# Two convolutions on one core: the last stage's matrices block diagonal over two channel groups instead of four, applied as pairs of 64x64 array tiles

## The chip, the cores and the metric

One core of one Trainium2 chip. The metric is the device time of one execution in microseconds (us). A kernel is timed several times in turn with the kernel before on the same chip. The profile of a run is of one execution; its span is about 2 us shorter than the time of the same run.

## The reference, cut to what matters

Two long convolutions over 2048 steps of 448 channels, one with a filter that has to be generated from 256 complex modes a channel (A), one with a given filter (B), mixed by a gate:

```python
def reference(A_u, A_A_re, ..., B_ssm_D, gate_w):
    ...
    K = jnp.einsum("dn,dnl,dn->dl", Cc, P, dB).real        # A: the filter from its modes
    y = irfft(rfft(u, 4096) * rfft(K, 4096))[:2048] + u * Dskip
    ...
    y = irfft(rfft(kv, 4096) * rfft(ssm_k, 4096))[:2048]   # B; kv: a short convolution of k, times v
    ...
    x = A_u
    g = _sigmoid((x * gate_w).sum(-1, keepdims=True))
    return g * a + (1 - g) * b
```

(The transforms and the paddings are written in short here; the cuts are marked with dots.)

## The kernel before

The 448 channels are worked in four quarters H of 112 (28 columns by 4 groups g). Each transform is a chain of small matrix stages on TensorE (PE): stage c spreads the input over 32 frequencies (`spread`, ps_c), stage 2 (`transform`, ps), a product of spectra on VectorE (DVE, zs and zsS times zsK), and back through stage a (ps_a into U) and stage b, the last, into ps_b. The filter of A is made in eight **filter blocks**, two for each quarter: powers of the modes multiplied and added on DVE (kg_P, kg_TQ, kg_TP), then summed over the modes on PE (pk). A **convolution step** carries one quarter of A or B through the stages. The program emits step after step with a filter block each; a scheduler with a model of its own then sets the order on each engine.

The stage in question, and how its matrices are built. `g` runs over the four groups of a quarter. Column block g of a 128x128 matrix (32 columns) is nonzero only in the 32 rows that carry the same group (every fourth row), so three quarters of the matrix are zeros:

```python
    def stage_b(self, pool, qt, hqt, k_col, mask):                 # once, early
        G = pool.tile([P, 64, 2, 4, 32], bf16, name="sb_G")
        for b0 in range(0, 64, 16):
            ...                                                    # phases, then ACT: v = sin(...)
            for g in range(4):
                nc.vector.tensor_scalar(out=G[:, b0:b0 + 16, :, g, :], in0=v[:], scalar1=mask[:, g:g + 1], scalar2=None, op0=ALU.mult)

def stage_b(nc, psum, G, U, consume, banks=2):                     # eight times
    n = 16 * banks
    for b0 in range(0, 64, n):
        pt = psum.tile([P, banks, 512], f32, name="ps_b", tag="ps")
        for i in range(n):
            b = b0 + i
            o = pt[:, i // 16, (i % 16) * NC:(i % 16 + 1) * NC]
            for r in range(2):
                nc.tensor.matmul(o, lhsT=G[:, b, r].rearrange("p g a -> p (g a)"), rhs=U[:, r, b], start=(r == 0), stop=(r == 1))
        consume(b0, n, pt[:, :, 0:448])        # DVE: ug (B) or ept and ug (A), from ps_b; for one quarter ACT: y
```

## Time and profile before

| | before |
|---|---|
| time, median of 3 | 326.08 us (326.0 to 326.8) |
| span of the profiled run | 323.5 us |
| mean granted PE clock | 0.800 |
| last kg_TP ends / copy of kg_S begins | 284.6 / 291.6 us |
| the eight ps_b stages, from first to last matmul | 28.7 us in all, 3.2 to 4.6 each |

How to read it: DVE is the busiest engine until the last filter block, so the time can be written as a **ledger of DVE**: what passes before the first filter operation (kg_P), DVE's work and idle time from there to the last kg_TP, and work and idle time in the tail behind it. The windows view: its columns are the stretch in us, its length, the busy time (and instructions) of PE, PE's weight loads, DVE, ACT and POOL, the granted clock, the DMA share and GB/s.

```profile
80.60:284.60 204.00, 160.99 (x4267) 148.48 (x4265) 193.18 (x377) 174.41 (x304) 9.42 (x1) 0.82 0.17 37
284.60:323.50 38.90, 19.22 (x565) 17.84 (x563) 11.82 (x22) 12.58 (x17) 0.00 (x0) 0.66 0.34 64
```

DVE idles 204.0 - 193.2 = 10.8 us in the stretch and 38.9 - 11.8 = 27.1 us in the tail. The chain that ended last, by line:

```profile
ACT zs L565 12%; PE ps_b L279 7%; PE pk L371 6%; ACT ET L481 6%; ACT U L565 5%; ACT zsK L565 5%; PE ps_c L215 5%; SPq L634 4%; POOL skraw L592 4%; PE ps L227 3%; SPq L587 3%; PE ps_a L265 3%; ACT ET L493 3%; SPq L631 2%; ACT ET L511 2%
```

### The profile page before, as it was taken

To read this page: it belongs to the slowest core of one execution; us is meant where nothing else is said; L and a number is where in the kernel's file an instruction comes from. 1 tells how busy PE (TensorE), PEld (TensorE's weight loads), DVE (VectorE), ACT (ScalarE), POOL (GpSimd) and SP (SyncE) were. 2 spreads that over 40 slices of the span, in tenths; PEclk is the share of its full clock that TensorE was granted. 3 is DMA by queue.
4 is the path that set the end of the run, shared out by engine and by line. 5 is a ranking of instruction groups with operands and counts; after the bars stand their busy time and mean duration, and the time that the engine had idled before them with its cause. 6 is when DMAs were issued, how large, how long until landed. Compare 5 with 4: busy or idle time off the path is not lost.

```text
span 323.5 us, 11944 instructions
## 1 busy us (share of the span) xinstructions
PE 225.5 (70%) x5286; PEld 197.4 (61%) x5286; DVE 277.2 (86%) x571; ACT 243.2 (75%) x395; POOL 34.6 (11%) x129
## 2 busy tenths in 40 slices
PE   0498617737278678699997857999774779966740
PEld 0144607237167568588886846998674678865740
DVE  7999999967999899979999998988999889942450
ACT  3655888779991799998989999689989474936600
POOL 9400002912000009000000000000000000000000
PEclk9999855796758767967997975899998559995765
DMA  6889999730000530050040015004000500040048
GB/s 129 137 188 152 165 164 168 239 59 0 2 0 4 117 57 3 5 158 2 4 102 19 4 45 116 3 4 97 22 2 4 115 3 4 12 108 2 2 91 140
DMA packets 53740, 21.41 MB, mean 66 GB/s; under 512 B 49080, under 2 KB 52024, under 8 KB 53688
## 3 DMA queue, kind: packets, MB, share of 16 engines
q1 hardware_dynamic: 48936, 19.47, 31.6%
q10 hardware_dynamic: 4560, 1.15, 2.0%
q8 instruction: 41, 0.67, 0.9%
q14 instruction: 11, 0.09, 0.1%
q0 software_dynamic: 192, 0.03, 0.1%
HBM read 10.09 MB, written 3.21 MB: 41 GB/s over the span
## 4 chain that ended last, share of the span: by engine, by line
ACT 39%; PE 26%; SPq 14%; DVE 9%; POOL 4%; issue 3%; DMA 3%; ACTq 0%; DVEq 0%; POOLq 0%
ACT zs L565 12%; PE ps_b L279 7%; PE pk L371 6%; ACT ET L481 6%; ACT U L565 5%; ACT zsK L565 5%; PE ps_c L215 5%; SPq L634 4%; POOL skraw L592 4%; PE ps L227 3%; SPq L587 3%; PE ps_a L265 3%; ACT ET L493 3%; SPq L631 2%; ACT ET L511 2%
## 5 line engine op out<-in xcount | busy, mean ns | idle before, releaser
L565 ACT CAST zs<-ps_c 128x1024 bf16<-128x1024 f32 (+1 forms) x48 | 42.5, 940 | 4.8 <-PE ps_c L215 4.7
L227 PEld LDWEIGHTS <-s_W 128*128 128x128 bf16 x480 | 34.4, 118 | 16.7 <-issue 14.2
L318 DVE TENSOR_TENSOR kg_P<-kg_TQ,ET 128x896 bf16<-128x896 bf16 (+1 forms) x64 | 43.8, 705 | 0.3
L565 ACT CAST zs<-ps 128x896 bf16<-128x896 f32 x48 | 41.4, 929 | 1.6 <-PE ps L227 1.5
L227 PE MATMUL ps<-zs,s_W 128*128 128x112 bf16 x384 | 32.2, 252 | 12.2 <-ACT zs L565 6.3
L371 PE MATMUL pk<-kg_TP,kg_TQ 128*21 128x32 bf16 x1792 | 30.3, 238 | 8.5 <-issue 6.3
L371 PEld LDWEIGHTS <-kg_TQ 128*21 128x21 bf16 x1792 | 27.8, 121 | 10.3 <-issue 9.6
L265 PE MATMUL ps_a<-sa_R,zs 128*128 128x128 bf16 x196 | 29.0, 240 | 6.8 <-ACT U L565 4.5
L592 POOL TENSOR_TENSOR skraw<-skraw,dB 128x28 bf16<-128x28 bf16 x4 | 23.3, 5816 | 94.9 <-DMA skraw<-in_B_ssm_k_dram 94.9
L565 ACT CAST U<-ps_a 128x1024 bf16<-128x1024 f32 (+2 forms) x32 | 29.3, 947 | 3.5 <-PE ps_a L253 1.8
L318 DVE TENSOR_TENSOR kg_P<-kg_TP,ET 128x1792 bf16<-128x1792 bf16 (+1 forms) x32 | 30.8, 963 | 0.0
L279 PEld LDWEIGHTS <-sb_G 128*128 128x128 bf16 x1024 | 27.9, 99 | 3.9 <-issue 3.6
L279 PE MATMUL ps_b<-U,sb_G 128*128 128x28 bf16 x1024 | 28.1, 179 | 2.9 <-ACT U L565 1.3
L265 PEld LDWEIGHTS <-zsS 128*128 128x128 bf16 x196 | 26.2, 153 | 5.2 <-issue 5.2
L265 PE MATMUL ps_a<-sa_R,zsS 128*128 128x128 bf16 x196 | 28.5, 239 | 0.0
L265 PEld LDWEIGHTS <-zs 128*128 128x128 bf16 x196 | 26.2, 152 | 2.6 <-DVE zs L286 1.7
L323 DVE TENSOR_TENSOR kg_TQ<-kg_P 128x896 bf16<-128x896 bf16 (+2 forms) x64 | 27.7, 442 | 0.2
L493 ACT ACTIVATE ET<-ks_ph 128x448 bf16<-128x448 int16 x40 | 23.8, 603 | 5.0 <-DVE ks_ph L489 4.0
L565 ACT CAST zsK<-ps_c 128x512 bf16<-128x512 f32 (+2 forms) x28 | 22.1, 798 | 7.0 <-PE ps_c L215 6.9
L215 PE MATMUL ps_c<-WcK,kg_KT 128*64 128x128 bf16 x224 | 19.9, 305 | 9.1 <-ACT zsK L565 5.8
L655 PE MATMUL ps_v<-kvt,scratch 128*128 128x448 bf16 x64 | 16.3, 387 | 13.5 <-DVE kvt L651 13.1
L215 PE MATMUL ps_c<-Wc,kv 128*64 128x128 bf16 x224 | 15.6, 321 | 14.1 <-DVE kv L680 7.8
(141 smaller groups left out, 481.4 us busy)
## 6 DMA issues: line engine op xcount, KB each, us to landing
zsS<-zs SPq DMA_DIRECT2D x16, 448.0 KB, 5.6
kt<-in_B_k_dram SPq DMA_DIRECT2D x16, 112.0 KB, 4.3
skraw<-in_B_ssm_k_dram SPq DMA_DIRECT2D x16, 112.0 KB, 3.6
vt<-in_B_v_dram SPq DMA_DIRECT2D x4, 448.0 KB, 6.8
uu<-in_A_u_dram SPq DMA_DIRECT2D x4, 448.0 KB, 8.7
xfd<-ks_hold SPq DMA_DIRECT2D x2, 672.0 KB, 6.9
ks_xf<-xfd SPq DMA_DIRECT2D x3, 336.0 KB, 3.0
out_dram<-ug SPq DMA_DIRECT2D x8, 112.0 KB, 4.8
```

The lines of the kernel that those rows point to most:

```text
L215: nc.tensor.matmul(pt[64 * r:64 * r + 64, i, :], lhsT=x, rhs=W[:, 128 * r:128 * r + 128], start=True, stop=True, tile_position=(0, 64 * r))
L227: nc.tensor.matmul(pt[:, i // 4, (i % 4) * n:(i % 4 + 1) * n], lhsT=W[:, k].rearrange("p r s -> p (r s)"), rhs=zs[:, k], start=True, stop= ...
L265: nc.tensor.matmul(pt[:, i, :], lhsT=t[:].rearrange("p k (g c) -> p (k g) c", g=4)[:, :, j + i], rhs=R[:, 128 * n:128 * n + 128], start=(n ...
L279: nc.tensor.matmul(o, lhsT=G[:, b, r].rearrange("p g a -> p (g a)"), rhs=U[:, r, b], start=(r == 0), stop=(r == 1))
L318: put(V.tensor_tensor(out=P4[:, i:i + m].rearrange("p n v c m -> p n v (c m)"), in0=in0, in1=in1, op=ALU.mult))
L323: put(V.tensor_tensor(out=T[:, dst:dst + v.shape[1] // 2].rearrange("p n v m -> p (n v) m"), in0=v[:, :, 0], in1=v[:, :, 1], op=ALU.add))
L371: nc.tensor.matmul(pt[32 * g:32 * g + NQ, hw, :].rearrange("p (i j) -> p i j", i=2), lhsT=TQ[:, :, c, m], rhs=rhs, start=(hf == 0 and c == 0),
L481: ex = nc.scalar.activation(dst, x, ACT.Exp, scale=float(e))
L493: sn = nc.scalar.activation(dst.rearrange("p b c m -> p b (c m)"), low16(ph[:].rearrange("p b c m -> p (b c m)")).rearrange("p (b x) -> p ...
L565: return nc.scalar.copy(dst, src)
L592: nc.gpsimd.tensor_tensor(out=raw[:, :, 0], in0=raw[:, :, 0], in1=dB[:, H * NC:(H + 1) * NC], op=ALU.add)
L655: nc.tensor.matmul(pt[:, i, 0:448], lhsT=ident, rhs=t[:, n, 4 * i:4 * i + 4, :].rearrange("p b l -> p (b l)"), start=(n == 0), stop=(n == 3))
```

## The change

The intent: not to build and load all of those zeros. With the four groups put into two halves h (two groups on partitions 0 to 63, two on 64 to 127), the halves never mix, so two of the four 64x64 blocks of the matrix are zero as a whole. The two others can run as independent tiles of the array, side by side, with half the matrix to build and to load. The cost is twice as many load and matmul instructions in the stage. Spectra (zs, zsS, zsK) are stored with the half outermost.

```diff
-        G = pool.tile([P, 64, 2, 4, 32], bf16, name="sb_G")
+        G = pool.tile([P, 64, 2, 2, 32], bf16, name="sb_G")
...
-            for g in range(4):
+            for g in range(2):
                 nc.vector.tensor_scalar(out=G[:, b0:b0 + 16, :, g, :], ...)
...
             for r in range(2):
-                nc.tensor.matmul(o, lhsT=G[:, b, r].rearrange("p g a -> p (g a)"), rhs=U[:, r, b], start=(r == 0), stop=(r == 1))
+                for h in range(2):
+                    q = slice(64 * h, 64 * h + 64)
+                    nc.tensor.matmul(o[q], lhsT=G[q, b, r].rearrange("p g a -> p (g a)"), rhs=U[q, r, b], start=(r == 0), stop=(r == 1),
+                                     tile_position=(64 * h, 64 * h))
...
-        zs = qt([P, 32, 4 * NC], "zs")
+        zs = qt([P, 2, 32, 2 * NC], "zs")
```

Cut: the same renaming of axes in `spread`, `transform`, `half_of`, `stage_a` and the copies, the spread matrix Wc built in two operations, and the columns of the mask.

More of the change, by code (lines that the diff above doesn't have):

```diff
@@ L109, in stage_c @@
         W = self.pool.tile([P, 256], bf16, name=name)
-        nc.vector.tensor_tensor(out=W[:].rearrange("p (n g) -> p n g", g=4), in0=v[:].unsqueeze(2).to_broadcast([P, 64, 4]),
-                                in1=maskg[:].unsqueeze(1).to_broadcast([P, 64, 4]), op=ALU.mult)
+        for h in range(2):
+            nc.vector.tensor_tensor(out=W[:].rearrange("p (r h k g) -> p h r k g", r=2, h=2, g=2)[:, h],
+                                    in0=v[:].rearrange("p (r k) -> p r k", r=2).unsqueeze(3).to_broadcast([P, 2, 32, 2]),
+                                    in1=maskg[:, 2 * h:2 * h + 2].unsqueeze(1).unsqueeze(1).to_broadcast([P, 2, 32, 2]), op=ALU.mult)
         return W
@@ L206, in col_of, with columns @@
         return self.sel[:, self.var[key]].rearrange("p a b -> p (a b)")
+def columns(zs):
+    return zs[:].rearrange("p h k (g c) -> p (h k g) c", g=2)
 def spread(nc, psum, W, zs, cols, groups, evac, room=8, tag="ps", at=0):
@@ L217, in spread @@
         n = len(whs)
-        evac(zs[:].rearrange("p k (g c) -> p (k g) c", g=4)[:, :, at + whs[0]:at + whs[0] + n], pt[:, 0:n].rearrange("p i kg -> p kg i"))
+        evac(columns(zs)[:, :, at + whs[0]:at + whs[0] + n], pt[:, 0:n].rearrange("p i kg -> p kg i"))
 def transform(nc, psum, W, zs, evac, ks=range(4)):
@@ L226, in transform @@
             k = 8 * kk + i
-            nc.tensor.matmul(pt[:, i // 4, (i % 4) * n:(i % 4 + 1) * n], lhsT=W[:, k].rearrange("p r s -> p (r s)"), rhs=zs[:, k],
+            nc.tensor.matmul(pt[:, i // 4, (i % 4) * n:(i % 4 + 1) * n], lhsT=W[:, k].rearrange("p r s -> p (r s)"), rhs=zs[:, :, k],
                              start=True, stop=True)
-        evac(zs[:, 8 * kk:8 * kk + 8].rearrange("p (i k) c -> p i (k c)", i=2), pt[:, :, 0:4 * n], kk % 2)
+        evac(zs[:, :, 8 * kk:8 * kk + 8].rearrange("p h (i k) c -> p i k h c", i=2),
+             pt[:, :, 0:4 * n].rearrange("p i (k h c) -> p i k h c", k=4, h=2), kk % 2)
 def half_of(zs, k0, k1, half):
-    return zs[:, k0:k1].rearrange("p k (g s c) -> p (k g) s c", g=4, s=2)[:, :, half]
+    return zs[:, :, k0:k1].rearrange("p h k (g s c) -> p h (k g) s c", g=2, s=2)[:, :, :, half]
 def transform_half(nc, psum, W, zs, evac, half):
@@ L244, in transform_half @@
             k0 = 16 * kk + 8 * i
-            evac(half_of(zs, k0, k0 + 8, half), pt[:, i, 0:448].rearrange("p (k c) -> p k c", c=CB), i)
+            evac(half_of(zs, k0, k0 + 8, half).rearrange("p h (k g) c -> p k h g c", g=2),
+                 pt[:, i, 0:448].rearrange("p (k h g c) -> p k h g c", k=8, h=2, g=2), i)
 def stage_a_half(nc, psum, U, R, terms, evac, half):
@@ L252, in stage_a_half @@
             for n, t in enumerate(terms):
-                nc.tensor.matmul(pt[:, i, :], lhsT=t[:].rearrange("p k (g c) -> p (k g) c", g=4)[:, :, j + i],
+                nc.tensor.matmul(pt[:, i, :], lhsT=columns(t)[:, :, j + i],
                                  rhs=R[:, 128 * n:128 * n + 128], start=(n == 0), stop=(n == 1))
@@ L264, in stage_a @@
             for n, t in enumerate(terms):
-                nc.tensor.matmul(pt[:, i, :], lhsT=t[:].rearrange("p k (g c) -> p (k g) c", g=4)[:, :, j + i],
+                nc.tensor.matmul(pt[:, i, :], lhsT=columns(t)[:, :, j + i],
                                  rhs=R[:, 128 * n:128 * n + 128], start=(n == 0), stop=(n == 1))
@@ L278, in stage_b, with products @@
             for r in range(2):
-                nc.tensor.matmul(o, lhsT=G[:, b, r].rearrange("p g a -> p (g a)"), rhs=U[:, r, b], start=(r == 0), stop=(r == 1))
+                for h in range(2):
+                    q = slice(64 * h, 64 * h + 64)
+                    nc.tensor.matmul(o[q], lhsT=G[q, b, r].rearrange("p g a -> p (g a)"), rhs=U[q, r, b], start=(r == 0), stop=(r == 1),
+                                     tile_position=(64 * h, 64 * h))
         consume(b0, n, pt[:, :, 0:448])
-def products(nc, X, S, Y, k0=0, k1=32):
-    fl = lambda t: t[:, k0:k1].rearrange("p k c -> p (k c)")
+def products(nc, X, S, Y):
+    fl = lambda t: t[:].rearrange("p h k c -> p (h k c)")
     for t in (S, X):
@@ L600, in swapped @@
     def swapped(zs, op=None):
-        swap = qt([P, 32, 4 * NC], "zsS")
+        swap = qt([P, 2, 32, 2 * NC], "zsS")
         for r in range(2):
@@ L662, in body @@
     W2 = cons.stage_2(cons.field("b2", 0, 63), [cons.field("o2%d" % r, 6, 1, -QUARTER, (1 + r) * QUARTER) for r in range(2)], kgp, wtc)
-    k_col, mask_b = cons.field("kB", 2, 31, 4.0, 1.0, pool=wp), cons.onehot("mgB", 4, cons.field("gB", 0, 3), 1.0 / 2048, pool=wp)
+    k_col, mask_b = cons.field("kB", 1, 31, 4.0, 1.0, pool=wp), cons.onehot("mgB", 2, cons.field("gB", 0, 1), 1.0 / 2048, pool=wp)
     R = cons.stage_a(cons.field("sA", 0, 63), [cons.field("oA%d" % r, 6, 1, HALF, (1 - r) * QUARTER) for r in range(2)])
@@ L714, in block @@
         if KA[H] is None:
-            KA[H] = qt([P, 32, 4 * NC], "zsK")
+            KA[H] = qt([P, 2, 32, 2 * NC], "zsK")
         S = kg.block(j, evac, kvl if j == 0 else None)
```

## The prediction

> **What bounds the kernel now.** I read the page first: busy shares, then the slices.
>
> ```profile
> PE 225.5 (70%) x5286; PEld 197.4 (61%) x5286; DVE 277.2 (86%) x571; ACT 243.2 (75%) x395; POOL 34.6 (11%) x129
> ...
> DVE  7999999967999899979999998988999889942450
> ...
> PEclk9999855796758767967997975899998559995765
> ```
>
> DVE is at nine tenths from slice 2 to slice 34 (8 to 283 us) and slack afterwards. So the kernel is two pieces: a stretch bound by DVE, which ends with the last operation of the last filter block, and a tail after it that is a chain through PE, ACT and DVE. The timelines of DVE and ACT give the border:
>
> ```profile
> 283.49 1.09 DVE L328 TENSOR_TENSOR kg_TP<-kg_TP,ET 128x1792 bf16<-128x1792 bf16 x1
> ...
> 291.63 0.53 ACT L565 CAST kg_S<-pk 128x448 bf16<-128x448 f32 x1 [5.31 <-PE pk L371]
> ```
>
> The last kg_TP ends at 284.6, the sums over it (kg_S) are copied out at 291.6, the span ends at 323.5: a tail of 38.9 us. The timed median is 326.1, 2.6 over the profiled span.
>
> The stage that changes is line 279. From the groups, and from PE's timeline and the windows for one stage at each clock:
>
> ```profile
> L279 PE MATMUL ps_b<-U,sb_G 128*128 128x28 bf16 x1024 | 28.1, 179 | 2.9 <-ACT U L565 1.3
> ...
> 250.37 3.57 PE L279 MATMUL ps_b<-U,sb_G 128*128 128x28 bf16 x128
> ...
> 279.83 3.36 PE L279 MATMUL ps_b<-U,sb_G 128*128 128x28 bf16 x128 [0.26 <-ACT zs L565]
> ```
> ```profile
> 279.80:283.20 3.40, 3.37 (x130) 3.33 (x129) 3.40 (x6) 2.85 (x4) 0.00 (x0) 1.00 0.15 34
> 250.40:253.90 3.50, 3.50 (x132) 3.46 (x135) 2.06 (x3) 1.97 (x3) 0.00 (x0) 0.50 0.33 70
> ```
>
> Take one matmul's duration off the stretch and divide by 127: (3.36-0.17)/127 = 25.1 ns at full clock, (3.57-0.19)/127 = 26.6 ns at half clock. Halving the clock hardly matters, so the 28 streamed columns are not the limit; a fixed cost per load and matmul is.
>
> PE's timeline also shows a limit that has nothing to do with the array, in the 21-column matmuls of the tail:
>
> ```profile
> 284.93 1.60 PE L371 MATMUL pk<-kg_TP,kg_TQ 128*21 128x32 bf16 x94
> 287.90 2.12 PE L371 MATMUL pk<-kg_TP,kg_TQ 128*21 128x32 bf16 x128 [1.38 <-issue]
> 291.36 0.23 PE L371 MATMUL pk<-kg_TP,kg_TQ 128*21 128x32 bf16 x2 [1.33 <-issue]
> ...
> q8 instruction: 41, 0.67, 0.9%
> ```
>
> Exactly 128 loads and 128 matmuls stand between two waits on "issue", and 0.67 MB in 41 packets is 16 KB a packet, about 256 instructions (10,572 load and matmul records over 41 packets). The waits look like PE waiting for its next packet of instructions. From wait to wait it took 287.90 to 291.36, 3.46 us: 13.5 ns an instruction, 27 ns a load and matmul. Faster bursts live from what was fetched before.
>
> **What the Trainium skill says.** "TensorEngine Tiling (Array Packing)", Restrictions: column tiling disables the fast weight load. The trace agrees as far as it can: the 64-column loads from skraw took 110 ns, the 128-column ones of this stage 96, so half the columns cost more, not less. The same page, Instruction Overhead: each matmul has an overhead of about 60 cycles, and one should not tile a dimension that is already small. 25.1 ns is 60 cycles of 2.4 GHz, which agrees; but matmuls that alternate between column tiles go below it (224 pk matmuls in 3.57 us, 15 ns each). "TensorE: Matmul & The Clock Gate", Part 1: the clock is either half or full, by recent activity; the windows above show 0.50 and 1.00. "GPSIMD Engine Reference", Specifications: GpSimd shares its SBUF interface with VectorE; here one POOL add of 128x28 took 11.4 us beside a saturated DVE (54.9 to 66.3).
>
> **The change, part by part.**
>
> (1) Matrices. sb_G loses 8 of 16 scaled copies:
>
> ```profile
> L155 DVE TENSOR_SCALAR sb_G<-sb_v,mgB 128x1024 bf16<-128x1024 bf16 x16 | 6.5, 472 | 0.0
> ```
>
> The timeline has eight of them in 3.24 us. DVE was busy 20.00 of 20 us from 40 to 60, so all of it comes off the path, and the POOL add behind it can end earlier as well: -3.2 us. The spread matrices take two small operations for one, early and tiny.
>
> (2) The stage itself: 1024 loads and matmuls become 2048, with the same 28 columns. Do the two 64x64 tiles run side by side? skraw's matmuls alternate between two column tiles with 128 columns each: 48 in 1.53 us at clock 1.00, (1.53-0.22)/47 = 27.9 ns, so 56 ns a pair, about the 53 ns that one alone needs to stream. Column tiles do overlap, and I take it that row-and-column tiles do. A pair then costs the load of 64 columns: the 14 ns between 96 and 110 are 32 more columns, so 64 take about 27 ns at full clock and 53 at half. Estimate for a stage of 128 pairs: 3.4 us at full clock (before 3.2), 6.8 at half (before 3.4). Independently, 512 instructions at 13.5 ns are 6.9 us once the fetched store is gone, and the new order puts 448 pk instructions right behind them in six of eight stages. I expect 4.5 to 6.5 us a stage, +2 on average: +15 us of PE over seven stages. PE has slack; I put 4 us of it on the path.
>
> (3) Copies, multiplies, swaps: the halves only move the outer index. Same elements, same stride of 28 in the loads of stage a, whole rows in the swap transfers, innermost runs of 56 instead of 448 in the copies from ps. ACT already writes runs of 8 at 1.04 us for 1024 elements, the same rate as 929 ns for 896. No cost.
>
> (4) The order. The scheduler places instructions by its own model, to which 256 matmuls are twice 128. The comparison of the instruction orders shows large moves. On PE the changes of tile shape go from 86 to 142 (transform and gather matmuls one by one alternately). (Each of the two convolutions, A and B, runs once per quarter of the channels: A1 is A's quarter 1. A filter block, kg_ and pk, makes half a quarter's filter for A.) On DVE each convolution step slips behind the filter blocks: before, the last filter block has in its midst the epilogue of A1 (two ept, two ug) and the products of A2; after, these stand behind the last kg_TP. That is 2x1.09+2x0.62+2x2.01 = 7.4 us of DVE work less in the first piece, but a whole convolution step more behind the last pk on PE and ACT.
>
> First piece: 284.6 - 3.2 - 7.4 - 6.6 (the waits of ug and ept on ps_b that later places remove: 3.6 and 3.0) + 4 (part 2) = 271 to 272.
> Tail: 38.9, plus the ACT copies that now stand between the last pk and its kg_S (zsK from ps_c 3.0, zsK from ps 4x0.93, kg_KT 0.56, zs from ps_c 3x1.04+0.63: 11 us), plus those after kg_S that stood before it (kg_KT 0.56, U 3.7, zs 4x0.93, y 1.9, zsK 2.2: 12 us), plus 1 for the slower last stage, whose four pieces are otherwise paced by DVE: 63 us, less some overlap.
> Sum: about 272 + 61 = 333 of span, 335 timed, +2.8%.
>
> **Rivals.** (a) Tiles fully parallel and supply no limit: the stage costs 25 ns a pair as before, and only the gain of 3.2 us and the order remain. If the tail's extra ACT work falls into its waits (ACT is busy only some 16 of the last 43 us), 322 to 326. For it: pk's 15 ns; against it: the waits on issue. (b) Tiles not overlapping, since both write one PSUM bank: 53 ns a pair at full clock, 107 at half, so 7 to 13 us a stage, PE becomes the bound: 345 to 360. Against it: the overlap of skraw's column tiles. (c) The clock: if sparsely used tiles count as less activity, more of the run falls to half clock, and every PE stage of the chain stretches: +5 to +10. (d) The order costs nothing because filter blocks and convolution steps only change places: 324 to 330.
>
> **Range and chances.** Early gain and hidden stage give 322; order, supply and clock together give 348. I take 335, range 324 to 347. Faster needs (a) and a tail that absorbs a step: 0.08. Within 2% (319.6 to 332.6) is (d), or half of the tail estimate: 0.35. Slower: 0.57.
>
> **What would show it.** Right: sb_G from 6.5 to about 3.3 us; 2048 ps_b matmuls, LDWEIGHTS near 110 ns; stages of 3.4 us only at full clock with a full store, else 5 to 7, with waits on issue in the ps_b and pk runs; about 49 instruction packets; last kg_TP near 272 and a tail of about 60 us with ACT densely busy. Wrong: stages of 3.3 us throughout (a), 7 us and more at full clock with no wait on issue (b), a last kg_TP as late as 285 (no gain of the first piece), or a tail still near 40 us.

## More of the kernel before

All stages share three PSUM buffers (tag "ps"), and every result goes through ScalarE (ACT) or DVE before a buffer is free again.

## The result, and the profile after

The changed kernel is correct and takes **362.72 us** (median of 4 runs, 360.48 to 364.02) against 326.42 us for the kernel before in the same rounds: ratio 1.110, 95% interval 1.105 to 1.115. A ratio is the mean time of one kernel's fast runs over the mean of the other's of the same rounds, so not quite the ratio of the medians quoted. The direction was predicted, the size was not: 362.7 lies outside 324 to 347.

The page of the changed kernel, the lines that answer to those shown of before (busy time and share of each engine; DVE and the clock in 40 slices; the instruction queue):

```profile
PE 247.6 (69%) x6310; PEld 215.4 (60%) x6310; DVE 275.2 (77%) x565; ACT 243.5 (68%) x395; POOL 19.2 (5%) x129
...
DVE  6999996879998996799996999999998110413440
...
PEclk9999856886566589867869996659698855985585
...
q8 instruction: 49, 0.80, 1.0%
```

DVE is dense until slice 31 and mostly idle in the last nine, where before it was mostly idle in the last five. 49 packets of instructions, as predicted. The groups of the stage and of its matrices (busy us and mean ns of one; idle before, releaser):

```profile
L289 PE MATMUL ps_b<-U,sb_G 64*64 64x28 bf16 x2048 | 44.7, 191 | 13.5 <-issue 9.1 <-ACT zs L576 2.9 <-ACT U L576 1.3
L289 PEld LDWEIGHTS <-sb_G 64*64 64x64 bf16 x2048 | 43.8, 128 | 14.7 <-issue 14.0
...
L157 DVE TENSOR_SCALAR sb_G<-sb_v,mgB 128x1024 bf16<-128x1024 bf16 x8 | 3.3, 476 | 0.0
```

sb_G is halved (3.3 us), a load of 64 columns takes 128 ns in the mean (128 columns took 99), and PE waits 9.1 us on "issue" within the stage. The ledger of the changed kernel:

```profile
79.20:276.80 197.60, 145.97 (x4254) 132.77 (x4254) 186.41 (x370) 147.89 (x270) 3.41 (x1) 0.77 0.14 32
276.80:358.70 81.90, 55.87 (x1581) 51.19 (x1579) 19.70 (x29) 38.46 (x50) 0.00 (x0) 0.67 0.24 47
```

The first kg_P comes 1.4 us earlier and the last kg_TP 7.8 us earlier (276.8), but the tail is 81.9 us instead of 38.9, and DVE idles 62.2 us of it. Where in the tail DVE waits is told by its timeline (start, duration, operation, and in brackets the idle time before it and what ended it):

```profile
284.32 1.09 DVE L753 TENSOR_TENSOR ept<-ps_b,gt 128x896 bf16<-128x896 f32 x1 [7.50 <-PE ps_b L289]
...
304.78 2.02 DVE L297 TENSOR_TENSOR zsS<-zsS,zsK 128x3584 bf16<-128x3584 bf16 x1 [15.86 <-ACT zsK L576]
...
318.99 0.62 DVE L773 TENSOR_TENSOR y<-y,gb 128x896 bf16<-128x896 bf16 x1 [10.25 <-ACT y L576]
```

Each is a convolution step's chain (PE, ACT, PE, DVE) with no filter block left to work on beside it.

### The profile page after: what moved, and what is told of

It is laid out like the page before. It is cut to its first block, busy times and chain, and to the rows that moved or that the text cites.

```text
span 358.7 us, 13990 instructions
## 1 busy us (share of the span) xinstructions
PE 247.6 (69%) x6310; PEld 215.4 (60%) x6310; DVE 275.2 (77%) x565; ACT 243.5 (68%) x395; POOL 19.2 (5%) x129
## 4 chain that ended last, share of the span: by engine, by line
ACT 27%; PE 25%; DVE 19%; SPq 14%; issue 6%; DMA 6%; DVEq 0%; ACTq 0%
ACT zs L576 9%; PE ps_b L289 7%; ACT zsK L576 6%; DVE kg_P L329 6%; PE pk L382 5%; PE ps_a L273 4%; PE ps_c L221 4%; SPq L598 4%; ACT U L576 4%; DMA zsS<-zs 3%; SPq L645 3%; SPq L642 3%; ACT ET L504 2%; PE ps L233 2%; DVE zsS L297 2%
## 5 line engine op out<-in xcount | busy, mean ns | idle before, releaser
L289 PE MATMUL ps_b<-U,sb_G 64*64 64x28 bf16 x2048 | 44.7, 191 | 13.5 <-issue 9.1
L289 PEld LDWEIGHTS <-sb_G 64*64 64x64 bf16 x2048 | 43.8, 128 | 14.7 <-issue 14.0
L233 PEld LDWEIGHTS <-s_W 128*128 128x128 bf16 x480 | 33.2, 115 | 22.5 <-issue 19.1
L233 PE MATMUL ps<-zs,s_W 128*128 128x112 bf16 x384 | 34.3, 245 | 16.7 <-ACT zs L576 9.3
L504 ACT ACTIVATE ET<-ks_ph 128x448 bf16<-128x448 int16 x40 | 23.2, 589 | 22.3 <-DVE ks_ph L500 19.6
L382 PE MATMUL pk<-kg_TP,kg_TQ 128*21 128x32 bf16 x1792 | 30.6, 238 | 11.0 <-issue 10.3
L273 PE MATMUL ps_a<-sa_R,zs 128*128 128x128 bf16 x196 | 31.3, 253 | 1.7 <-ACT zs L576 1.2
L273 PE MATMUL ps_a<-sa_R,zsS 128*128 128x128 bf16 x196 | 30.8, 251 | 0.0
L273 PEld LDWEIGHTS <-zs 128*128 128x128 bf16 x196 | 27.1, 154 | 1.6 <-DVE zs L297 0.6
L273 PEld LDWEIGHTS <-zsS 128*128 128x128 bf16 x196 | 27.3, 155 | 1.2 <-issue 1.2
L221 PE MATMUL ps_c<-Wc,kv 128*64 128x128 bf16 x224 | 15.9, 317 | 16.5 <-ACT zs L576 7.2
L221 PEld LDWEIGHTS <-kv 128*64 128x64 bf16 x224 | 15.4, 220 | 17.2 <-issue 10.1
L666 PE MATMUL ps_v<-kvt,scratch 128*128 128x448 bf16 x64 | 16.0, 375 | 13.8 <-DVE kvt L662 13.3
```

The source lines that it names most:

```text
L221: nc.tensor.matmul(pt[64 * r:64 * r + 64, i, :], lhsT=x, rhs=W[:, 128 * r:128 * r + 128], start=True, stop=True, tile_position=(0, 64 * r))
L233: nc.tensor.matmul(pt[:, i // 4, (i % 4) * n:(i % 4 + 1) * n], lhsT=W[:, k].rearrange("p r s -> p (r s)"), rhs=zs[:, :, k], start=True, st ...
L273: nc.tensor.matmul(pt[:, i, :], lhsT=columns(t)[:, :, j + i], rhs=R[:, 128 * n:128 * n + 128], start=(n == 0), stop=(n == 1))
L289: nc.tensor.matmul(o[q], lhsT=G[q, b, r].rearrange("p g a -> p (g a)"), rhs=U[q, r, b], start=(r == 0), stop=(r == 1), tile_position=(64 * ...
L382: nc.tensor.matmul(pt[32 * g:32 * g + NQ, hw, :].rearrange("p (i j) -> p i j", i=2), lhsT=TQ[:, :, c, m], rhs=rhs, start=(hf == 0 and c == 0),
L504: sn = nc.scalar.activation(dst.rearrange("p b c m -> p b (c m)"), low16(ph[:].rearrange("p b c m -> p (b c m)")).rearrange("p (b x) -> p ...
```

## The experiments

Two causes are mixed in the changed kernel: the stage itself is longer, and the scheduler, to whose model 256 matmuls are twice 128, puts the convolution steps behind the filter blocks. (layout_only, below, keeps the old order, so it is the tiles, with their halved matrices, that move it; which of the two it is in the scheduler's model, no run separates.) To take them apart, the order on every engine is pinned: the order that the scheduler chose for one kernel is written down as a list, and each instruction of another kernel is tied to its predecessor in that list (the two matmuls of a tile pair count as one entry). The traces bear it out: tiles_old_order has its instructions in the order of before, and full_new_order in the order of the changed kernel, on every engine, but for some neighbouring ps_c matmuls whose recorded starts change places. The pinning helper shifts line numbers: line 279 of before is a line in the 350s or 360s there.

```diff
         body(tc, *args)
+        in_order(tc, ORDERS)   # per engine: add_manual_dep(next, previous, NoSync) along the list
```

### The layout alone: layout_only

The two-half layout, but one 128x128 matrix padded with zeros in the place of two tiles. The scheduler itself gives it the order of before.

```diff
-                for h in range(2):
-                    ... two 64x64 tiles
+                nc.tensor.matmul(o, lhsT=G[:, b, r].rearrange("p g a -> p (g a)"), rhs=U[:, r, b], start=(r == 0), stop=(r == 1))
```

> Spectra in two halves and matrices block diagonal over two quarters, but kept as one 128x128 matrix with zeros off the blocks; the scheduler gives it the order of the kernel before by itself. If the layout costs nothing: 325 to 328 us. If the copies with runs of 56 or the split reads of the transforms cost something: 330 us or more, with longer copies from ps.

Measured: 325.90 us (4 runs) against 326.19, ratio 1.000 (0.996 to 1.004). The layout costs nothing; what follows is tiles and order.

### Tiles and order apart: tiles_old_order, full_new_order

tiles_old_order is the changed kernel in the order of before; full_new_order is the kernel before, with its 128x128 matrices, in the order of the changed one.

> The changed kernel, with every engine's instructions pinned to the order that the scheduler had made of the kernel before (a pair of tile matmuls in the place of one matmul). Theory O (the new order of the instructions is most of the +36 us): the stage alone adds some 8 us on the path and the early DVE saving takes 3 off, so 328 to 336 us. Theory S (the slower stage itself is on the path, in whatever order): 350 us or more.

> The kernel before, whole 128x128 matrices, pinned to the order that the scheduler made of the changed kernel. Theory O: 342 to 355 us, with the last filter block done near 275 us and a tail of 70 us or more. Theory S: at most 335 us.

Measured, with layout_only and the changed kernel as the other corners:

| | old order | new order |
|---|---|---|
| one 128x128 matrix | 325.90 (ratio 1.000) | 351.14 (1.076, 1.071 to 1.082) |
| two 64x64 tiles | 355.42 (1.089, 1.081 to 1.097) | 362.72 (1.110, 1.105 to 1.115), before 326.42. It was run at another time. |

Both theories were half right: each cause alone costs most of the loss, 29.5 us for the tiles and 25.2 us for the order, and together they cost 36.8 (36.3 against the kernel before of its own call), not 54.7. The ledgers show where. First full matrices in the new order, then tiles in the old order:

```profile
80.70:280.80 200.10, 136.94 (x3628) 123.97 (x3627) 186.44 (x370) 148.41 (x270) 3.37 (x1) 0.74 0.14 31
280.80:349.50 68.70, 46.87 (x1194) 43.21 (x1191) 19.59 (x28) 37.86 (x50) 0.00 (x0) 0.85 0.29 56
```
```profile
78.70:310.30 231.60, 181.68 (x5143) 167.75 (x5142) 193.81 (x377) 173.31 (x302) 9.47 (x1) 0.75 0.15 34
310.30:353.50 43.20, 23.17 (x719) 21.54 (x718) 11.87 (x22) 13.86 (x18) 0.00 (x0) 0.62 0.31 56
```

| profiled run, us | before first kg_P | stretch: DVE busy + idle | tail: DVE busy + idle | span |
|---|---|---|---|---|
| before | 80.6 | 193.2 + 10.8 | 11.8 + 27.1 | 323.5 |
| full_new_order | 80.7 | 186.4 + 13.7 | 19.6 + 49.1 | 349.5 |
| tiles_old_order | 78.7 | 193.8 + 37.8 | 11.9 + 31.3 | 353.5 |
| after | 79.2 | 186.4 + 11.2 | 19.7 + 62.2 | 358.7 |

DVE's work from the first kg_P on is the same everywhere within 1.1 us (205.0 to 206.1), so nearly all of the difference is idle time of DVE. The order puts it into the tail (+22.0 there, +2.9 in the stretch). The tiles in the old order put it into the stretch (+27.0, and 4.2 in the tail). With both, the filter blocks run ahead and no longer wait for the slow stage (stretch +0.4); the stages' delay is then met only where three of them stand in the tail. By these ledgers, that is why the costs do not add.

### How the longer stage reaches the end: tiles_big_G, tiles_B_only

tiles_big_G: tiles_old_order with all sixteen scaled copies of sb_G. tiles_B_only: that, with tiles in the four stages of B and the full matrix in the four of A.

```diff
-                nc.tensor.matmul(o[q], lhsT=G[q, b, r].rearrange(...), ...)              # G: 2 groups
+                nc.tensor.matmul(o[q], lhsT=G[q, b, r, 2 * h:2 * h + 2].rearrange(...), ...)  # G: 4 groups, zeros elsewhere
...
+                if not tiled:   # tiles_B_only: the stages of A
+                    nc.tensor.matmul(o, lhsT=G[:, b, r].rearrange("p g a -> p (g a)"), rhs=U[:, r, b], start=(r == 0), stop=(r == 1))
+                    continue
```

> Pairs of tiles in the old order as in tiles_old_order, but the matrices are built with all 16 scaled copies, so this undoes the saving in sb_G alone. If the saving is worth what it moved the first kg_P there (1.9 us), 355.4 + 2 = 357 us, last kg_TP near 312. If it was eaten by later waits, 355 to 356. If it is worth its full 3.2 us of DVE time (as the prediction had it), 358 to 359.

> As tiles_big_G, but only the four stages of convolution B use pairs of tiles, the four of A use the full 128x128 matrix. In tiles_old_order the B stages had lengthened by 2.2, 4.3, 3.9 and 5.3 us (15.7 in all), the A stages by 14.8. Theory: in the old order each microsecond of the stage is on the path, so 326.2 + 15.7 + 0 to 1 = 341 to 344 us, with 28 to 30 us for the sum of stage times less 15. Rival: the early stages have slack and only the late ones (A) reach the end: 327 to 334. Rival: there is a threshold, any lengthening pushes a whole step behind: 350 and more.

Measured: tiles_big_G 355.54 us, ratio 1.092 (1.086 to 1.099), which can't be told from tiles_old_order's 1.089 (1.081 to 1.097): the two differ by about 1 us, give or take 3. So whether the saving of 3.2 us in the matrices reaches the end is left open. tiles_B_only 341.98 us, +16.7 over before, ratio 1.049 (1.044 to 1.054), as the first theory had it. Its eight stages take 45.4 us in the trace from first to last matmul of each, 16.7 more than before. So in the old order the stage's length passes to the end at about one to one: 59.0 us of stages in tiles_old_order (+30.3) for +29.2 us of time. That ps_b was on the chain with 7% of the span before had said as much. In the new order the chain says the opposite; here it is from the page of full_new_order, with ps_b at 2%:

```profile
DVE kg_P L391 11%; ACT zs L638 8%; ACT zsK L638 5%; PE ps_a L338 4%; DVE kg_TQ L396 4%; PE ps_c L288 3%; ACT U L638 3%; ACT ET L554 3%; ACT ET L566 3%; DVE zsS L359 2%; PE ps_b L352 2%; DVE zs L359 2%; PE ps L300 2%; PE pk L444 2%; DMA zsS<
```

And there the tiles cost 11.6 us (351.14 to 362.72), not 29.5.

### What sets the stage's length: lower_tile_half, column_tiles, twice_128

lower_tile_half (wrong, relative error 0.44: the lower tile works only for r = 0) has 192 tile matmuls a stage, not 256. column_tiles has pairs of 128 rows by 64 columns. twice_128 has the full matrix, each output done in two runs of 14 columns, so 256 full loads and matmuls a stage. All in the old order.

```diff
                 for h in range(2):
+                    if h and r: continue                                                                   # lower_tile_half
-                    nc.tensor.matmul(o[q], lhsT=G[q, b, r]..., rhs=U[q, r, b], tile_position=(64 * h, 64 * h), ...)
+                    nc.tensor.matmul(o[q], lhsT=G[:, b, r, 2 * h:2 * h + 2]..., rhs=U[:, r, b], tile_position=(0, 64 * h), ...)   # column_tiles
+                    nc.tensor.matmul(o[:, 14 * h:14 * h + 14], lhsT=G[:, b, r]..., rhs=U[:, r, b, 14 * h:14 * h + 14], ...)       # twice_128
```

> Wrong on purpose: tiles in the old order, but the lower tile multiplies only in the first of its two steps, 192 tile matmuls a stage in place of 256. If the two tiles run side by side and the 64-column load sets the pace, a stage takes as long as with all 256 (the upper tile still has 128 loads). If the number of instructions sets it, a stage takes three quarters.

> The old order, the 128-column matrices, and each step as a pair of column tiles of 128 rows by 64 columns (zero rows included), in place of 64 by 64: the loads have 64 columns as in the change, without row tiling. Theory (the 64-column load sets the pace): a pair takes 32 ns at full clock and 53 at half, stages net 4.3 to 4.8 and 6.8 to 7.1 us, 352 to 358 us in all. Rival (the row tiling costs it): a pair comes down to 25 to 28 ns, stages of 3.3 to 3.6 us where there is no wait on issue.

> The old order and the full 128x128 matrix, but each output column range is done in two halves of 14 columns, so that every matrix is loaded twice: as many instructions as with tiles, without tiles. Theory: a full load and matmul takes 25 to 27 ns at either clock, so 256 take 6.4 to 6.8 us at full clock too, and as the instructions are as many, the waits on issue in the stages (13 us in tiles_old_order, none before) come as well: 355 to 362 us. If the waits on issue stay away, they are of the tiles and not of the number of instructions.

One run each, of unknown state, so these times carry no interval: lower_tile_half 342.67 us, column_tiles 360.06 (352 to 358 expected), twice_128 356.31 (before 325.9 to 326.2). PE's timeline, half a stage at half clock, in tiles_old_order, lower_tile_half, column_tiles and twice_128, in this order:

```profile
142.31 3.59 PE L363 MATMUL ps_b<-U,sb_G 64*64 64x28 bf16 x128
```
```profile
142.54 3.59 PE L365 MATMUL ps_b<-U,sb_G 64*64 64x28 bf16 x96
```
```profile
144.27 3.59 PE L364 MATMUL ps_b<-U,sb_G 128*64 128x28 bf16 x128 [0.18 <-ACT zs L662]
```
```profile
144.03 3.56 PE L365 MATMUL ps_b<-U,sb_G 128*128 128x14 bf16 x128
```

128 tile matmuls are 64 pairs in 3.59 us, (3.59 - 0.19)/63.5 = 53.5 ns a pair. Taking away every second matmul of the lower tile changes nothing (96 in the same 3.59 us): the tiles do run side by side, and the upper tile's own load and matmul sets the pace. Rows do not matter: 128-row column tiles take the same. And at half clock 128 full matrices take the same 3.56 us. From all starts in the traces, tiles come every 26.7 ns at half clock and 15.9 ns at full clock, full matrices every 26.7 and 25.1 ns. In lower_tile_half, the upper tile's matmuls come every 53 ns at half clock and 31 ns at full clock, so the tile's own pace, and not the number of instructions, sets the length of a pair at both clocks. A pair thus costs 53 ns at half clock and 32 at full, against 27 and 25 for the one matrix that it replaces.

The second part is the supply of instructions. In twice_128, without any tile, PE waits on issue within the stages too:

```profile
148.38 0.56 PE L365 MATMUL ps_b<-U,sb_G 128*128 128x14 bf16 x15
150.23 3.18 PE L365 MATMUL ps_b<-U,sb_G 128*128 128x14 bf16 x113 [1.28 <-issue]
...
168.65 3.37 PE L365 MATMUL ps_b<-U,sb_G 128*128 128x14 bf16 x128 [0.78 <-issue]
172.65 3.32 PE L365 MATMUL ps_b<-U,sb_G 128*128 128x14 bf16 x119 [0.63 <-issue]
```

It waits 6.2 us there in all, tiles_old_order 11.6, column_tiles 13.8, and lower_tile_half, with three quarters of the matmuls, 1.0 (before, with half of them, 0.6). So the waits come with the number of instructions, and more of them where the array works them off faster, as tiles at full clock do.

### Is it only DVE standing at a fixed place? tiles_late_epilogue, full_late_epilogue

In tiles_old_order DVE waits 28.5 us for ps_b (ug 16.2, ept 12.3). If it merely comes too early, the waiting multiplies can come later. On DVE alone they were moved behind 4 us of other work; full_late_epilogue is the same move with full matrices.

```diff
-    DVE: ..., ug<-ps_b, (4 us of other work), ...
+    DVE: ..., (4 us of other work), ug<-ps_b, ...       # likewise ept<-ps_b and its ug; PE, ACT, POOL, SP as before
```

> tiles_old_order with one thing moved: on DVE the multiplies that take up the last stage's results (ug and ept from ps_b, with the ug behind ept; not those of the last quarter) come later by 4 us of other DVE work. PE, ACT, POOL and SP keep the old order. In tiles_old_order DVE stood 28.5 us at these multiplies, waiting for PE (before: 11.0). Theory: the lengthened stage costs time because DVE comes to a fixed place and stands there while filter work would be ready, so most of these waits (some 17 us) go: 335 to 345 us. Rival: PE's own chain sets the pace and DVE's wait only shows it; then the wait moves to another operation: 350 to 357 us.

> The control: the kernel before (full matrices) with the same move on DVE. Its waits of ug and ept on ps_b are 11.0 us, of which some 6 stand before the last filter block; 320 to 325 us if they go and nothing takes their place (then it would be the fastest kernel so far), 325 to 328 if they are paid elsewhere, more if the buffers that come free 4 us later hold up PE.

Measured: 366.65 us, ratio 1.125 (1.121 to 1.129), so 11 us **worse** than without the move, and 332.33 us for the control, ratio 1.020 (1.017 to 1.023), worse by 6 (beyond the noise, though not clearly by the 2% at which runs here are called slower). My theory falls, and the rival was too mild. The waits of DVE (engine, operation, what it waited for: us in total, times, longest), first tiles_old_order, then tiles_late_epilogue:

```profile
DVE ug L819 <- PE ps_b L363: 16.2, 7, 4.1
DVE ept L829 <- PE ps_b L363: 12.3, 5, 4.6
DVE ET L593 <- ACT ET L580: 11.9, 5, 3.9
```
```profile
DVE ET L593 <- ACT ET L580: 36.3, 7, 8.2
DVE zsS L373 <- ACT zsK L652: 8.3, 2, 8.1
DVE zsS L373 <- DMA zsS<-zs: 7.0, 3, 2.8
DVE ept L829 <- PE ps_b L363: 6.5, 3, 4.6
```

The waits at ug and ept nearly went (6.5 us left), and DVE then stood 36.3 us at ET, behind ACT. What DVE does with ps_b is itself a link of the chain: it feeds what ACT delivers next. The shared ps buffers are one such link, and the trace shows it. PE waited for ug and ept, which free a buffer, before matmuls that read neither of them; first tiles_old_order, then tiles_late_epilogue:

```profile
PE ps_c L295 <- DVE ept L829: 0.8, 1, 0.8
```
```profile
PE ps_c L295 <- DVE ept L829: 4.0, 1, 4.0
PE ps_c L295 <- DVE ug L819: 2.7, 1, 2.7
PE ps L307 <- DVE ug L819: 1.2, 1, 1.2
```

At 155.79 us, for instance, the moved ug begins. Its end starts PE's ps_c at 156.92, for which ACT then waits 2.9 us, and DVE waits 5.7 us for ACT's ET at 169.83. How much of the 11 us goes this way is not shown: no run changed the number of buffers, and the control's trace has no such wait of PE for its 6 us.

### What the order costs: full_late_old, full_late_new, full_new_to_block_3, full_new_to_block_4

All with full matrices. full_late_old takes the new order for all that the old one has done by the end of the sixth filter block, and the old order from there. full_late_new is the reverse. full_new_to_block_3 and _4 are full_late_old with the seam after the third and the fourth block.

```diff
-    ORDERS = the new order
+    ORDERS = what the old order has done by the end of block 6 (3, 4), in the new order; then the rest, in the old order
```

> Full 128x128 matrices, all engines pinned: everything that the old order has done by the end of the sixth filter block comes in the new order, what is left (the last two filter blocks and the rest) in the old order, so the lagging convolution step is caught up before the end. Theory: what the new order costs is that one convolution step more stands behind the last filter block; the lag itself costs nothing on the way: 326 to 331 us, with a tail of 38 to 43 us behind the last kg_TP. Rival: the new order loses a little at every step through waits of DVE: 337 to 345.

> The other way round: everything that the new order has done by the end of the sixth filter block comes in the old order, the rest in the new order, so the last two blocks run ahead of the convolution steps as in full_new_order. Theory (the step behind the last block is the whole cost): 346 to 352 us, with last kg_TP at 278 to 285 and a tail near 68. Rival (gradual loss): 333 to 341.

> Full matrices; the new order up to what the old one has done by the end of its third filter block, the old order from there. At that point both orders have done two of the eight last stages. Theory (the cost falls due at once, for one convolution step without a filter block beside it): nothing is behind yet, so 325 to 330 us. Rival (gradual, by the share of the way: 3 of 8 blocks of +22 to +25): 333 to 336 us.

> The same up to the end of the fourth filter block, by which the old order has done the third last stage and the new one has not, so the step has to be caught up alone. Theory: DVE idle there for some 15 us and 340 to 349 us in all, as in full_late_old. Rival (gradual, 4 of 8): 336 to 339 us.

Measured: full_late_old 347.80 us, ratio 1.068 (1.063 to 1.072); full_late_new 346.16, 1.063 (1.056 to 1.069), in the range expected of it, with the last kg_TP at 275.8 (278 to 285 expected) and a tail of 70.7; full_new_to_block_3 336.78, 1.035 (1.031 to 1.040); full_new_to_block_4 341.55, 1.050 (1.047 to 1.052). I had thought that catching up before the end would be free. In full_late_old the tail is back at 38.2 us, but here is the stretch in which the lagging step is caught up, and DVE in it:

```profile
234.90:260.00 25.10, 22.09 (x441) 20.75 (x440) 8.56 (x8) 20.22 (x27) 0.00 (x0) 0.83 0.18 39
```
```profile
250.36 1.09 DVE L804 TENSOR_TENSOR ug<-ps_b,ug 128x896 bf16<-128x896 f32 x1 [11.97 <-PE ps_b L351]
```

DVE idles 16.5 of 25.1 us. PE and ACT do the convolution step that had been put off, and no filter work is there for DVE. So a put-off convolution step costs this wherever it stands, in the tail or at the seam; what made it free before was a filter block beside it. The idle time of the block at the seam, from the windows of full_new_to_block_3, full_new_to_block_4 and full_late_old:

```profile
151.90:195.40 43.50, 36.12 (x820) 33.19 (x817) 34.83 (x68) 35.40 (x52) 0.00 (x0) 0.84 0.11 24
```
```profile
182.30:225.30 43.00, 35.20 (x940) 33.01 (x941) 29.24 (x46) 38.19 (x68) 0.00 (x0) 0.88 0.23 54
```
```profile
234.90:285.70 50.80, 42.01 (x989) 39.17 (x989) 31.66 (x53) 36.39 (x55) 0.00 (x0) 0.80 0.18 39
```

That is 8.7, 13.8 and 19.1 us, where before had 0.1 to 1.7 us in the same blocks. The debt grows with the way: +11.2, +16.0 and +22.6 us of time for three, four and six blocks in the new order, +25.0 for all eight (each against the kernel before). Neither theory of the last two runs was right as put, though full_new_to_block_4 fell into the range of the first (340 to 349): there is a debt already after three blocks, although both orders have done two last stages by then, and it is not in proportion to the blocks either. None of these runs beats the kernel before; the best, layout_only, equals it.

## Why the prediction was wrong

**Right.** DVE bounds the first piece and a tail follows; the scaled copies fell to 3.3 us; 49 packets; loads of 64 columns are slower than those of 128 (128 against 99 ns; 110 was forecast); column tiles overlap (two of skraw take 56 ns at full clock, where one 128x128 matmul of ps_a, with as many columns streamed, takes 63); a pair takes about 53 ns at half clock (at full clock 27 predicted, 32 measured); waits on issue in ps_b and pk; the steps slip behind the blocks; layout and copies cost nothing (layout_only). Rival (a) (tiles as cheap as before) and (d) (the order is free) are refuted by the two pinned kernels. Rival (b) came nearest in size (345 to 360) for the wrong reason: the tiles do overlap (lower_tile_half). Of (c), the clock fell from 0.800 to 0.764; no run isolates what that cost.

The 53 ns was partly luck. The prediction gets 27 and 53 ns for a load of 64 columns by calling the 14 ns between the two loads "32 more columns", but these loads have 64 and 128 columns, and nothing shown says where 32 comes from. That the upper tile's own load and matmul set the pace is shown only by lower_tile_half.

**Wrong, first piece: 271 to 272 predicted, 276.8 measured.** "-3.2" for sb_G became -1.4 at the first kg_P. "-7.4" for moved work was -6.8 (193.2 to 186.4 busy). The failed step is "-6.6 (the waits of ug and ept ...) + 4 (part 2)", -2.6 in all: DVE's idle time rose by 0.4. Waits that the moved operations left were replaced by others, in full_new_order already (+2.9).

**Wrong, tail: 61 predicted, 81.9 measured; this is most of the miss.** Two terms failed. The step "38.9, plus the ACT copies", +23 less some overlap, is +29.8 in full_new_order (38.9 to 68.7). The added convolution step was priced as the ACT work in it. It is a chain through PE, ACT and DVE with nothing beside it: ACT, forecast densely busy in the tail, was busy 38.5 of 81.9 us. At the last kg_TP, PE in full_new_order was still busy with the put-off step's stages, so the sums began 8 us later, where before they began 0.3 us later:

```profile
285.47 3.44 PE L352 MATMUL ps_b<-U,sb_G 128*128 128x28 bf16 x128
288.85 2.11 PE L444 MATMUL pk<-kg_TP,kg_TQ 128*21 128x32 bf16 x128
291.70 1.61 PE L444 MATMUL pk<-kg_TP,kg_TQ 128*21 128x32 bf16 x96 [0.74 <-issue]
```

"Plus 1 for the slower last stage" is +13.2 (68.7 to 81.9). Three stages stand in the tail, not one, and take 17.2 us where full matrices take 9.8, which is 7.4; and the instructions of the stage in front starve pk, a further 2.6 us: from the beginning of ps_b to the end of pk it is 7.8 us above (285.47 to 293.31) and 12.0 us in the changed kernel (282.08 to 294.11), where the stage itself took only 1.6 us more:

```profile
282.08 5.04 PE L289 MATMUL ps_b<-U,sb_G 64*64 64x28 bf16 x256
287.66 2.11 PE L382 MATMUL pk<-kg_TP,kg_TQ 128*21 128x32 bf16 x128 [0.54 <-issue]
292.49 1.62 PE L382 MATMUL pk<-kg_TP,kg_TQ 128*21 128x32 bf16 x96 [2.71 <-issue]
```

The remaining 3.2 us I have not traced; the clock in the tail was 0.67 against 0.85.

**Mis-sized: the stage.** "+2 on average", 4.5 to 6.5 us a stage, was 53.8 us in eight stages against 28.4 in the same order, +3.2 each, 6.7 on average. And "PE has slack; I put 4 us of it on the path" was wrong as a way of reasoning. In the old order all of it is on the path (tiles_old_order, tiles_B_only); in the new order none of it shows in the first piece and all of what is in the tail does. PE's share of busy time said slack; the chain view, with ps_b at 7%, said path.

**Open.** By which links the stage's delay comes back to DVE in the old order (in tiles_old_order PE waited only 0.8 us for a ps buffer that DVE held), and what the scheduler would do with a truthful cost for tile pairs: the best order for tiles was not searched, only the old and the new one run.

## What to carry to other kernels

Halving the zeros in a matrix by pairs of tiles doubles loads and matmuls, and with 28 streamed columns a pair of 64-column tiles cost 53 ns at half clock and 32 at full, against 27 and 25 for the one matrix with zeros in it: measure a pair before trading it for a matrix. Whether a longer stage would show was told here by the chain that ended last (ps_b 7% in the old order, 2% in the new), and not by PE's share of busy time. Where a scheduler sets the order, a change of instruction count is also a change of order: pin the old order to see the two apart, and price a step that loses its partner as its whole chain.

## What the Trainium skill lacked or had wrong

- "Runtime: NRT & Kernel Launch", Instruction fetch mechanics, has instructions come in blocks of 16 KiB (256 instructions), which the traces agree with (0.80 MB in 49 packets), but calls the cost of a block mostly hidden, with dispatch slower than the refill. In dense runs of small matmuls it is not: PE waited 19.4 us on issue in ps_b and pk of the changed kernel (9.1 + 10.3), up to 2.7 us at once, and in such runs a packet came every 3.4 to 4.0 us.
- "TensorE: Matmul & The Clock Gate", Part 1, says that start-to-start never drops below about 25 ns. Full matrices agree (25.1 ns at full clock); matmuls that alternate between two tiles do not: 15.9 ns on average, for 64x64 as for 128x64. The sentence lacks the exception for tiles; the page's own Part 3 has tiles start about 4 ns apart, which the traces bear out (at full clock the gaps alternate between about 4 and 28 ns).
- No page puts a number on a pair of 64-column tiles against the one full matrix that it replaces: 32 ns against 25.1 at full clock and 53 against 26.7 at half clock, with 28 streamed columns.
